# Both filter products in one operation, and twenty weight tiles beside the first batch's length-47 steps

## The chip, the cores and the metric

The kernel runs on one core of a Trainium2 chip. A core has five engines with instruction streams of their own: TensorE (PE, with its weight loads listed as PEld), VectorE (DVE), ScalarE (ACT), GpSimd (POOL) and SyncE (SP). They work on tiles in SBUF, a memory of 128 partitions; TensorE writes its results to banks of a second memory, PSUM. Transfers between these and the main memory (DMA) are issued from the queues of SP, ACT and POOL. The metric is the device time of one execution in microseconds (us); the time of before is the median of six runs.

## The reference

Two blocks follow each other on x of shape (8, 3008, 256), all in float32 except the four mixer weights, which arrive as float64.

```python
X = np.fft.rfft(x, axis=1)                      # 1505 frequencies along the sequence
Y = X * (filt_r + 1j * filt_i)[None]            # a complex filter for each frequency and channel
x = np.fft.irfft(Y, n=3008, axis=1).astype(np.float32)
xt = x.transpose(0, 2, 1)
h = np.maximum(xt @ w_tok1, 0.0) @ w_tok2       # token mixing: 3008 -> 256 -> 3008
u = x + h.transpose(0, 2, 1)
h2 = np.maximum(u @ w_ch1, 0.0) @ w_ch2         # channel mixing: 256 -> 1536 -> 256
out = (u + h2).astype(np.float32)
```

## The kernel before

**The transform.** The length 3008 is split as 64 x 47. A forward transform of a batch has twelve units of the length-64 part (`a_unit`, a matrix product with a table `wa`) and then 32 steps of the length-47 part, one for each k2. In a step `b_unit(k)` multiplies by the step's table and leaves 128 rows of frequencies in PSUM: real parts in rows 0 to 63, imaginary parts in rows 64 to 127. Then DVE applies the filter, and `bi_unit(k)` applies the inverse table of length 47 and sends the result through ACT (the copy t at L520) to the scratch tensor `g_tmp` in main memory. The inverse of the length-64 part is folded into the mixer: `w_tok1` is multiplied by that inverse when it is loaded (`w1`), and the second token product adds it by way of `wai`.

**The filter products.** A complex product needs re*fr, im*fr, -im*fi and re*fi. The tile `filt` holds filt_r in part 0 (rows 0 to 63, doubled into rows 64 to 127) and filt_i in part 1. In the first batch DVE makes p1 = ps * fr over 128 rows (L502), and p2 with the halves swapped: p2[re] = -ps[im] * fi (L503) and p2[im] = ps[re] * fi (L504). `bi_unit` then multiplies both p1 and p2 by the same inverse table and lets PSUM add them. In the later groups, of two batches each, DVE adds p1 and p2 itself.

**The order.** The order of all work is written out by hand. The first batch is transformed alone (`dft(GROUPS[0])`), before there is anything to mix; the other seven go in groups beside the mixer of the batches before. The first batch's `a_unit`s take the first 20 us, then come transposes on DVE, then the 32 steps. ACT doubles the filter of the next pair of steps at every odd step (`filt_double`, L226), ahead of the copy t of that step. The filter of a pair (c) is six transfers, on POOL's queue except for c = 1 and 2, which go through SP's.

**The weights.** 40 tiles of float64 weights are turned to float32: 12 of w_tok1 (tiles 0 to 11, 512 columns), 16 of w_tok2 (tiles 12 to 27, 377 columns), 12 of the channel weights. Each tile is a generator with stages: start the load; an ACT operation (L246); four DVE operations (L248, L249, L251, L253), which split a number into a top and a rest; and then the sum of the two. For w_tok1 and the first `BY_PE` tiles of w_tok2 PE forms the sum, as two products with the table `wai_t` or the identity (L285, L286), and ACT copies it out (L288); for the others DVE adds (L274). `convert()` ends the oldest tile, gives the next one its ACT operation and starts loads up to six tiles ahead (`fill`). A buffer of a load comes free when the DVE operations of its old tile are done.

Before the change `convert()` is called 12 times beside the 32 steps and 16 times after them. Between these, after the sixth w_tok2 tile, come the token sums of batch 0 (`token_sums`, 96 instructions, L566), which need all of w1 and all of the batch read back from `g_tmp` (`t4_load`, L560). After the last w_tok2 tile the mixer begins: `token_relu` (L572), `u_part` (L583, L588), `v_steps` (L601), then the loop `mix`.

Of the kernel before, what the change touches and what calls it, by code (L numbers as in the profile page):

```python
# [10 lines left out]
FP32 = mybir.dt.float32  # L11
I64 = mybir.dt.int64
U32 = mybir.dt.uint32
AF = mybir.ActivationFunctionType
# [29 lines left out]
MT = 6  # L44
NG = 8
PARTS = (0, 64, 112)
BY_PE = 6
EARLY = 12
GROUPS = ((0,), (1, 2), (3, 4), (5, 6), (7,))

# [74 lines left out]
def kernel(  # L125
# [64 lines left out]
    wai_t = glob.tile([P, P], FP32, name="wai_t")  # L190
    ident = h1p.tile([P, P], FP32, tag="h1", name="ident")

    filts = [glob.tile([P, 2, KC, D], FP32, name="filt%d" % i) for i in range(FB)]
    w1 = glob.tile([P, A, DT], FP32, name="w1")

# [12 lines left out]
    def filt_load(c, first):  # L208
        t, k0 = filts[c % FB], c * KC


        q = nc.gpsimd if first and c not in (1, 2) else nc.sync
        for src, i, p0 in ((filt_r, 0, 0), (filt_i, 1, HALF)) + (() if first else ((filt_r, 0, HALF),)):
            q.dma_start(t[p0:p0 + A, i], raw(src, k0, [[64 * D, A], [D, KC], [1, D]]))
            lo = p0 + 32
            if k0 == 0:
                q.dma_start(t[lo:lo + A, i, 0, :], raw(src, 32, [[64 * D, A], [1, D]]))
            k = max(k0, 1)

            for j0, n in ((0, 16), (16, A - 1 - 16)):  # L220
                q.dma_start(t[lo + j0:lo + j0 + n, i, k - k0:KC, :],
                            raw(src, 64 * (j0 + 1) - k, [[64 * D, n], [-D, k0 + KC - k], [1, D]]))

    def filt_double(c):
        t = filts[c % FB]
        nc.scalar.copy(out=t[HALF:P, 0], in_=t[0:HALF, 0])  # L226

# [8 lines left out]
    def halves(st, n, pair):  # L238

        words = [st.bitcast(t).rearrange("p (n w) -> p n w", w=2)[:, 0:n] for t in (U32, FP32)]  # L240
        lo, hi, hi_f = words[0][:, :, 0], words[0][:, :, 1], words[1][:, :, 1]
        top, rest = (v[:, 0:n] for v in pair)
        top_i, rest_i = top.bitcast(U32), rest.bitcast(U32)


        nc.scalar.activation(out=top, in_=hi_f, func=AF.Copy, scale=2.0 ** -112)  # L246
        yield
        nc.vector.tensor_scalar(out=top_i, in0=top_i, scalar1=3, scalar2=None, op0=ALU.logical_shift_left)  # L248
        nc.vector.scalar_tensor_tensor(out=top_i, in0=hi, scalar=0x80000000, in1=top_i,  # L249
                                       op0=ALU.bitwise_and, op1=ALU.bitwise_or)  # L250
        nc.vector.tensor_scalar(out=rest_i, in0=top_i, scalar1=0xFF800000, scalar2=None, op0=ALU.bitwise_and)  # L251

        nc.vector.scalar_tensor_tensor(out=rest, in0=lo, scalar=2.0 ** -52, in1=rest, op0=ALU.mult, op1=ALU.mult)  # L253
        yield top, rest
# [9 lines left out]
    def rounded(st, n, parts, late):  # L264
        if late:

            pair = (p1p.tile([P, 512], FP32, tag="p1", name="top"), p2p.tile([P, 512], FP32, tag="p2", name="rest"))
        else:
            pair = spare_pair()
        h = halves(st, n, pair)  # L270
        yield next(h)
        top, rest = next(h)
        for src, dst in parts:
            nc.vector.tensor_tensor(out=dst, in0=src(top), in1=src(rest), op=ALU.add)  # L274
# [17 lines left out]
    def w1_load(i):  # L292
        st = stage(512)
        rows = moe_w_tok1.rearrange("(n2 n1) t -> n2 n1 t", n1=N1)
        q = nc.sync if i < EARLY else nc.gpsimd
        last = 2 * i + 2 == A
        if last:
            nc.gpsimd.memset(st.bitcast(U32)[HALF:P, 512:1024], 0)
        for h in range(2):
            n = 1 if last and h else 2  # L300
            lo = h * A + 2 * i
            q.dma_start(st[h * HALF:(h + 1) * HALF, 0:n * DT].rearrange("p (a t) -> p a t", t=DT),
                        rows[:, lo:lo + n, :])
        yield

        h = halves(st, 512, spare_pair())
        yield next(h)
        on_chip(wai_t, *next(h), 512, [(lambda v: v, w1[:, 2 * i:2 * i + 2, :].rearrange("p a t -> p (a t)"))])

    def w2_load(i):  # L310

        t, g = divmod(i, N2 // NG)
        n = NG * N1

        more = g + 1 < N2 // NG
        st = stage(512)
        nc.gpsimd.dma_start(st[:, 0:n + more], moe_w_tok2[ts(t, P), ds(g * n, n + more)])
        yield
        dst = w2[:, t].rearrange("p (a h n2) -> p h n2 a", h=2, n2=HALF)[:, :, ds(g * NG, NG), :]

        def some(h, nh, w):
            return (lambda v: bass.AP(tensor=v.tensor, offset=v.offset + h * A, ap=[v.ap[0], [A, nh], [N1, NG], [1, w]]),
                    dst[:, h:h + nh, :, 0:w])

        parts = [some(0, 2, A)] if more else [some(0, 1, A), some(1, 1, A - 1)]
        if i < BY_PE:
            h = halves(st, n + more, spare_pair())
            yield next(h)
            on_chip(ident, *next(h), n + more, parts)
        else:  # L330
            yield from rounded(st, n + more, parts, False)
# [23 lines left out]
    def wc2_load(i):  # L355
# [5 lines left out]
        def tile_of(dh):  # L361
# [9 lines left out]

    tiles = ([w1_load(i) for i in range(A // 2)] + [w2_load(i) for i in range(TC * N2 // NG)]
             + [wc1_load(c * (DC // 512), False) for c in range(DH)] + [f(i) for f, i in LAST])
    begin, copy, end = iter(tiles), iter(tiles), iter(tiles)

    def advance(it):
        s = next(it, None)
# [6 lines left out]

    def convert():

        ended[0] += 1
        while behind and behind[0][0] < ended[0] - 2:
            behind.pop(0)[1]()
        advance(end)  # L390
        advance(copy)
        fill(6)
# [46 lines left out]
    def dft(bs):  # L439
# [44 lines left out]
        def b_unit(k):  # L484
            tag = ("b", "pg")[k % 2] if first else free_bank()
            if not first:
                held.append(tag)
            ps = bank(tag).rearrange("p (b d) -> p b d", b=2)[:, 0:nb, :]
            t2 = turned[:, k, :].unsqueeze(1) if first else t2s[k // KC][:, k % KC]
            nc.tensor.matmul(ps, wbs[k // WC][0:P if first else KR, k % WC, 0:P], t2, start=True, stop=True)  # L490
            re, im = slice(0, HALF), slice(HALF, P)
            t = filts[k // KC % FB]
            fr = t[:, 0, k % KC, :].unsqueeze(1).to_broadcast([P, nb, D])
            fi = t[im, 1, k % KC, :].unsqueeze(1).to_broadcast([HALF, nb, D])
            p1 = p1p.tile([P, 2 if first else nb, D], FP32, tag="p1", name="p1")
            if first:
                p1, p2 = p1[:, 0:1], p1[:, 1:2]
                prods[k] = (p1, p2)
            else:
                p2 = p2p.tile([P, nb, D], FP32, tag="p2", name="p2")  # L500
                prods[k] = (p1,)
            nc.vector.tensor_tensor(out=p1, in0=ps, in1=fr, op=ALU.mult)  # L502
            nc.vector.scalar_tensor_tensor(out=p2[re], in0=ps[im], scalar=-1.0, in1=fi, op0=ALU.mult, op1=ALU.mult)  # L503
            nc.vector.tensor_tensor(out=p2[im], in0=ps[re], in1=fi, op=ALU.mult)  # L504
            if not first:
                nc.vector.tensor_tensor(out=p1, in0=p1, in1=p2, op=ALU.add)

        def bi_unit(k):

# [1 line left out]
            ps = bank("acc" if first else held.pop(0)).rearrange("p (b d) -> p b d", b=2)[:, 0:nb, :]  # L511
            parts = prods.pop(k)
            for i, p in enumerate(parts):
                nc.tensor.matmul(ps[0:KR], wbs[k // WC][:, k % WC, P:], p, start=(i == 0), stop=(i == len(parts) - 1))  # L514
            c, r = divmod(k, KC)
            if r == 0:
                where, tag = (p2p, "p2") if first and c % 3 == 2 else (t3p, "t3")
# [14 lines left out]
        yield  # L532
        if first:
            filt_double(0)
        for k in range(K2 + 1):
            if k < K2:
                b_unit(k)
# [8 lines left out]
                        table_load(k // KC + 4)  # L546
                if first and k % KC == KC - 1 and k + 1 < K2:
                    filt_double(k // KC + 1)
            if k >= 1:
                bi_unit(k - 1)  # L550
            yield
# [241 lines left out]
    with tc.manual_schedule():  # L793
        nc.sync.dma_start(wa0, wa0_d)
        nc.vector.memset(turned[:, A:K2, :], 0.0)
        for t in filts:
            nc.vector.memset(t, 0.0)
        rounds = 0
        second = dft(GROUPS[1])
        for i, _ in enumerate(dft(GROUPS[0])):  # L800
            if i == 0:
# [8 lines left out]
                    for t, src in ((wa, wa_d), (wai, wai_d), (ident, ident_d)):  # L810
                        nc.scalar.dma_start(t, src)
            elif k >= 0:
                if (k + 1) * (A // 2) // K2 > k * (A // 2) // K2:
                    convert()
                    rounds += 1

                if 19 <= k < 25:
                    t4_load(0, k - 19, 0, PARTS[1])
                elif k == 25:
                    next(second)  # L820
                elif k in (30, 31):
                    for c in range(3):
                        t4_load(0, 3 * (k - 30) + c, PARTS[1], PARTS[2])
# [3 lines left out]
        both = wcp.tile([P, 2, JP, 7, P], FP32, tag="wc", name="wc")  # L827

        chan.extend((both[:, 0], both[:, 1]))
        for i in range(rounds, A // 2 + TC * N2 // NG):  # L830
            convert()
            if i - rounds < XB:
                next(second)
            if i == A // 2 + BY_PE - 1:
                sum_up()
                acc = token_sums(0)
        h1s[0] = token_relu(acc)
        for dh in range(DH):
            convert()
# [59 lines left out]
```

## Time and profile before

| | |
|---|---|
| median of 6 runs | 2577.82 us (2576.47 to 2579.71) |
| profiled execution | 2579.51 us, its span 2577.7 us |
| busy over the span | PE 97%, DVE 70%, ACT 27%, POOL 20% |
| mean granted TensorE clock | 0.994 |
| first length-47 step to the last one's copy | 30.5 to 108.4 us |
| token sums of batch 0 | 122.6 to 143.5 us |
| first sums of the mixer (v, L601) | 155.0 us |

The profile is one execution on the chip. Engine rows with 40 digits give the busy share of 40 equal slices in tenths; a table by stages gives each engine's busy time and instruction count in a window, the granted clock, the mean busy share of 16 DMA engines and GB/s. A row of a group names a line, an engine, an operation, output and input with their shapes and a count; behind it stand busy us, mean ns of one, and the engine's idle time before these instructions with what ended it. A row of the timeline gives start, length, engine, line and instruction, and in brackets the idle time before it. Waits are listed as the waiting engine and line, what it waited for, us in all, times, and the longest.

### The profile page before, as it was taken

How to read it: one execution, taken by the hardware profiler on the slowest of the kernel's cores; microseconds unless marked ns; L12 is line 12 of the kernel's file. 1: busy time of each engine (PE TensorE's matmuls, PEld its weight loads, DVE VectorE, ACT ScalarE, POOL GpSimd, SP SyncE). 2: the span in 40 equal slices, each digit the busy share in tenths (PEclk: the TensorE clock that was granted, in tenths of full speed). 3: DMA queues.
4: the chain of work that ended last, by engine and by line, in shares of the span. 5: the costliest groups of instructions: out<-in, count | busy, mean ns of one | idle time of the engine just before them, and what ended most of it. 6: DMA issues, size and time to landing. Idle time of an engine off the chain costs nothing.

```text
span 2577.7 us, 31460 instructions
## 1 busy us (share of the span) xinstructions
PE 2502.7 (97%) x10952; PEld 1999.6 (78%) x10952; DVE 1815.4 (70%) x3458; ACT 691.9 (27%) x1347; POOL 527.5 (20%) x968
## 2 busy tenths in 40 slices
PE   6979999999999999999999999999999999999998
PEld 3557666888778777887888777788888888888887
DVE  7897888466585887745665888746678576647676
ACT  3533222122222222222221222213222122212222
POOL 4563111111211121112121111211211121211212
PEclk8999999999999999999999999999999999999999
DMA  9964333212322232203232233212222121100000
GB/s 212 231 205 146 96 104 96 86 58 92 99 85 63 81 92 62 80 25 92 88 93 73 79 85 86 82 28 65 85 82 77 51 62 53 25 9 8 17 12 21
DMA packets 153775, 205.21 MB, mean 80 GB/s; under 512 B 34128, under 2 KB 105074, under 8 KB 153616
## 3 DMA queue, kind: packets, MB, share of 16 engines
q1 hardware_dynamic: 82752, 114.46, 15.8%
q0 software_dynamic: 30912, 41.12, 6.7%
q10 hardware_dynamic: 39952, 47.61, 5.8%
q8 instruction: 87, 1.43, 0.2%
q14 instruction: 72, 0.59, 0.1%
HBM read 131.23 MB, written 71.83 MB: 79 GB/s over the span
## 4 chain that ended last, share of the span: by engine, by line
PE 79%; DVE 13%; DMA 3%; issue 2%; ACT 1%; POOL 1%; SPq 0%; ACTq 0%; DVEq 0%; POOLq 0%
PE ps_po L657 27%; PE ps_pg L623 16%; PE ps_pg L639 12%; PE ps_acc L583 4%; PE ps_acc L566 3%; PE ps_b L583 3%; PE ps_b L566 2%; DVE t L601 2%; DVE hh L601 2%; PE ps_acc L588 2%; PE ps_acc L514 2%; PE ps_b L430 2%; PE ps_b L490 2%; DVE u L601 1%; PE ps_acc L490 1%
## 5 line engine op out<-in xcount | busy, mean ns | idle before, releaser
L601 DVE TENSOR_TENSOR hh<-ps_pg,s 128x512 f32<-128x512 f32 (+3 forms) x864 | 482.0, 585 | 613.1 <-ACT s L626 612.5
L702 POOL DMA_DIRECT2D out_dram<-r x757 | 409.8, 550 | 1950.8 <-ACT hh L644 925.9
L644 ACT ACTIVATE hh<-hh 128x512 f32<-128x512 f32 (+1 forms) x576 | 347.9, 621 | 1113.9 <-DVE hh L601 1113.9
L657 PE MATMUL ps_po<-t,wc 128*128 128x256 f32 (+1 forms) x2304 | 537.0, 376 | 5.7 <-DVE t L601 4.7
L657 PEld LDWEIGHTS ps_po<-t,wc 128*128 128x128 f32 x2304 | 435.2, 190 | 132.2 <-issue 52.1
L657 PE MATMUL ps_po<-hh,wc 128*128 128x256 f32 (+1 forms) x1728 | 413.2, 375 | 2.9 <-POOL wc L340 1.5
L623 PE MATMUL ps_pg<-v,wc 128*128 128x256 f32 (+1 forms) x1728 | 413.4, 375 | 0.2
L657 PEld LDWEIGHTS ps_po<-hh,wc 128*128 128x128 f32 x1728 | 327.4, 190 | 42.1 <-POOL wc L340 1.9
L623 PEld LDWEIGHTS ps_pg<-v,wc 128*128 128x128 f32 x1728 | 326.9, 190 | 40.8 <-DVE v L601 3.2
L639 PE MATMUL ps_pg<-u,wc 128*128 128x256 f32 (+1 forms) x1152 | 293.3, 377 | 5.1 <-DVE hh L601 4.7
L601 DVE TENSOR_TENSOR t<-t,hh 128x256 f32<-128x256 f32 (+1 forms) x576 | 242.0, 420 | 19.8
L639 PEld LDWEIGHTS ps_pg<-u,wc 128*128 128x128 f32 x1152 | 215.8, 190 | 41.7 <-DVE hh L601 14.9
L601 DVE TENSOR_TENSOR s<-ps_pg,hh 128x512 f32<-128x512 f32 (+1 forms) x288 | 196.1, 681 | 30.3 <-DVE hh L601 0.5
L601 DVE TENSOR_TENSOR t<-hh 128x512 f32<-128x512 f32 (+1 forms) x288 | 192.4, 668 | 0.6 <-ACT hh L644 0.6
L623 PE MATMUL ps_pg<-u,wc 128*128 128x256 f32 (+1 forms) x576 | 169.8, 376 | 0.0
L639 PE MATMUL ps_pg<-v,wc 128*128 128x256 f32 (+1 forms) x576 | 169.1, 375 | 0.0
L626 ACT COPY s<-ps_pg 128x256 f32<-128x256 f32 (+1 forms) x288 | 106.0, 368 | 156.1 <-PE ps_pg L623 152.9
L639 PEld LDWEIGHTS ps_pg<-v,wc 128*128 128x128 f32 x576 | 108.5, 190 | 13.5 <-DVE s L601 0.4
L623 PEld LDWEIGHTS ps_pg<-u,wc 128*128 128x128 f32 x576 | 102.8, 191 | 19.4 <-issue 11.0
L583 PE MATMUL ps_acc<-w,h 128*128 128x512 f32 (+1 forms) x228 | 106.3, 588 | 3.5 <-DVE w L274 2.8
L514 PE MATMUL ps_acc<-p,wb 128*96 128x256 f32 (+1 forms) x256 | 96.6, 478 | 13.2 <-ACT t L520 7.3
L566 PE MATMUL ps_b<-t,w 128*128 128x256 f32 x384 | 83.8, 380 | 1.3 <-ACT t L520 1.3
(104 smaller groups left out, 2267.6 us busy)
## 6 DMA issues: line engine op xcount, KB each, us to landing
g_tmp<-t ACTq DMA_DIRECT2D x128, 192.0 KB
out_dram<-r POOLq DMA_DIRECT2D x698, 32.0 KB, 1.8
x<-in_x_dram SPq DMA_DIRECT2D x173, 128.0 KB
z_tmp<-t ACTq DMA_DIRECT2D x84, 256.0 KB
t<-z_tmp SPq DMA_DIRECT2D x112, 192.0 KB
t<-g_tmp SPq DMA_DIRECT2D x42, 512.0 KB
wb<-wbi_t SPq DMA_DIRECT2D x80, 224.0 KB
filt<-in_filt_r_dram SPq DMA_DIRECT2D x130, 48.0 KB
```

The lines of the kernel that those rows point to most:

```text
L430: nc.tensor.matmul(ps, wa0 if b == 0 else wa, xs.pop((b, c)).rearrange("p a d -> p (a d)"), start=True, stop=True)
L490: nc.tensor.matmul(ps, wbs[k // WC][0:P if first else KR, k % WC, 0:P], t2, start=True, stop=True)
L514: nc.tensor.matmul(ps[0:KR], wbs[k // WC][:, k % WC, P:], p, start=(i == 0), stop=(i == len(parts) - 1))
L566: nc.tensor.matmul(acc[:, t, :], w1[:, a, ts(t, P)], t4[b, a // TC4][:, a % TC4, :], start=(a == 0 and t == 0), stop=(a == A - 1 and t == ...
L583: nc.tensor.matmul(ps[:, 0:w], h1[:, t, ts(dh, P)], w2[:, t, ds(m * 512, w)], start=(t == 0), stop=False)
L601: nc.vector.tensor_tensor(out=out, in0=in0, in1=in1, op=op)
L623: nc.tensor.matmul(ps[:, 0:hw], chan[0][:, jp, n, :], mov, start=True, stop=True)
L626: nc.scalar.copy(out=s[:, 0], in_=g[0][:, 0, 0:hw])
L639: nc.tensor.matmul(ps[:, 0:hw], chan[0][:, jp, n, :], mov, start=True, stop=True)
L644: nc.scalar.activation(out=hs, in_=hs, func=AF.Relu)
L657: nc.tensor.matmul(po[i][:, j, 0:hw], chan[1][:, jp, n, :], mov, start=(jp == 0 and first == 1), stop=(jp == JP - 1 and last == 1))
L702: q.dma_start(rows[g, e, :, ds(h * A + 4 * m, n)], blocks[ts(g, CW), h, e, 0:n])
```

## The change

1. In the first batch one DVE operation makes both filter products: ps, read twice by a broadcast, times both parts of the filter tile, over 128 rows and 2 x 256 columns. For that filt_i is loaded into rows 0 to 63 like filt_r, and `filt_double` copies both parts (64x1024 instead of 64x512).
2. The swap and the sign that p2 had are put into a second inverse table, `turn_i`, that ACT makes from the first with two operations for each pair of steps (`table_turn`), ahead of the copy t of every odd step. `bi_unit` multiplies the second part by it. `turn_i` shares its buffer with the tile `s` of the mixer.
3. The four DVE operations of a tile are split into two stages of two operations. Beside the 32 steps 20 tiles (`IN_B`) are converted, in half stages, instead of 12; eight are left for after the loop.
4. PE forms the sum for 4 tiles of w_tok2 instead of 6. The token sums are issued before the conversions that follow the loop, not after the sixth of them, and the two `a_unit`s of the second group before the token sums.
5. The filter of c = 2 is loaded through POOL's queue instead of SP's.

```diff
-BY_PE = 6
+BY_PE = 4
+IN_B = 20
...
-        q = nc.gpsimd if first and c not in (1, 2) else nc.sync
-        for src, i, p0 in ((filt_r, 0, 0), (filt_i, 1, HALF)) + (() if first else ((filt_r, 0, HALF),)):
+        q = nc.gpsimd if first and c != 1 else nc.sync
+        for src, i, p0 in ((filt_r, 0, 0), (filt_i, 1, 0 if first else HALF)) + (() if first else ((filt_r, 0, HALF),)):
...
     def filt_double(c):
         t = filts[c % FB]
-        nc.scalar.copy(out=t[HALF:P, 0], in_=t[0:HALF, 0])
+        nc.scalar.copy(out=t[HALF:P], in_=t[0:HALF])
+
+    turn_i = sp.tile([P, 4, WC, KR], FP32, tag="s", name="turn_i")
+
+    def table_turn(g, wb):
+        wi, to = wb[:, :, P:], turn_i[:, g % 4]
+        nc.scalar.copy(out=to[0:HALF], in_=wi[HALF:P])
+        nc.scalar.activation(out=to[HALF:P], in_=wi[0:HALF], func=AF.Copy, scale=-1.0)
...
         nc.vector.scalar_tensor_tensor(out=top_i, in0=hi, scalar=0x80000000, in1=top_i,
                                        op0=ALU.bitwise_and, op1=ALU.bitwise_or)
+        yield
         nc.vector.tensor_scalar(out=rest_i, in0=top_i, scalar1=0xFF800000, scalar2=None, op0=ALU.bitwise_and)
...
-    begin, copy, end = iter(tiles), iter(tiles), iter(tiles)
+    begin, copy, middle, end = (iter(tiles) for _ in range(4))
...
     def convert():
+        advance(middle)
+        convert_end()
+
+    def convert_end():
         ended[0] += 1
...
             if first:
-                p1, p2 = p1[:, 0:1], p1[:, 1:2]
-                prods[k] = (p1, p2)
-            else:
-                p2 = p2p.tile([P, nb, D], FP32, tag="p2", name="p2")
-                prods[k] = (p1,)
+                nc.vector.tensor_tensor(out=p1, in0=ps.to_broadcast([P, 2, D]), in1=t[:, :, k % KC, :], op=ALU.mult)
+                prods[k] = (p1[:, 0:1], p1[:, 1:2])
+                return
+            p2 = p2p.tile([P, nb, D], FP32, tag="p2", name="p2")
+            prods[k] = (p1,)
...
-                nc.tensor.matmul(ps[0:KR], wbs[k // WC][:, k % WC, P:], p, start=(i == 0), stop=(i == len(parts) - 1))
+                wi = turn_i[:, k // WC % 4, k % WC] if i else wbs[k // WC][:, k % WC, P:]
+                nc.tensor.matmul(ps[0:KR], wi, p, start=(i == 0), stop=(i == len(parts) - 1))
...
         if first:
             filt_double(0)
+            table_turn(0, wbs[0])
...
                 if first and k % KC == KC - 1 and k + 1 < K2:
                     filt_double(k // KC + 1)
+                    table_turn(k // KC + 1, wbs[k // KC + 1])
...
             elif k >= 0:
-                if (k + 1) * (A // 2) // K2 > k * (A // 2) // K2:
-                    convert()
-                    rounds += 1
+                while half < 2 * IN_B * (k + 1) // K2:
+                    if half % 2:
+                        convert_end()
+                    else:
+                        advance(middle)
+                    half += 1
...
-        for i in range(rounds, A // 2 + TC * N2 // NG):
+        for _ in range(XB):
+            next(second)
+        acc = token_sums(0)
+        for _ in range(A // 2 + TC * N2 // NG - IN_B):
             convert()
-            if i - rounds < XB:
-                next(second)
-            if i == A // 2 + BY_PE - 1:
-                sum_up()
-                acc = token_sums(0)
         h1s[0] = token_relu(acc)
```

More of the change, by code (lines that the diff above doesn't have):

```diff
@@ L270, in rounded @@
         h = halves(st, n, pair)
+        yield next(h)
         yield next(h)
@@ L307, in w1_load @@
         yield next(h)
+        yield next(h)
         on_chip(wai_t, *next(h), 512, [(lambda v: v, w1[:, 2 * i:2 * i + 2, :].rearrange("p a t -> p (a t)"))])
@@ L327, in w2_load @@
             h = halves(st, n + more, spare_pair())
+            yield next(h)
             yield next(h)
@@ L504, in b_unit @@
             nc.vector.tensor_tensor(out=p2[im], in0=ps[re], in1=fi, op=ALU.mult)
-            if not first:
-                nc.vector.tensor_tensor(out=p1, in0=p1, in1=p2, op=ALU.add)
+            nc.vector.tensor_tensor(out=p1, in0=p1, in1=p2, op=ALU.add)
         def bi_unit(k):
@@ L797 @@
             nc.vector.memset(t, 0.0)
-        rounds = 0
+        half = 0
         second = dft(GROUPS[1])
```

## The prediction

> **What bounds the kernel now.** I read the page first, then the first 260 us by stage, then the waits, the chain of waits and each engine's timeline there. The page says where a change to the first batch can pay:
>
> ```profile
> span 2577.7 us, 31460 instructions
> ...
> PE   6979999999999999999999999999999999999998
> ...
> DVE  7897888466585887745665888746678576647676
> ...
> DMA  9964333212322232203232233212222121100000
> ```
>
> From about 200 us on TensorE (PE) is full; this work the change does not touch, so it can only start earlier or later. The profiled execution took 2579.51 us, 1.8 more than its span, and lies 1.7 above the median of 2577.82; I work in differences and subtract them from the median. The stages of interest are the loop of 32 length-47 steps (30.5 to 108.4) and the stretch from it to the mixer's first sums (155.0). The columns are length, then busy time of PE, PEld, DVE, ACT and POOL, granted clock, DMA share, GB/s:
>
> ```profile
> 30.50:108.40 77.90, 69.08 (x234) 40.94 (x235) 66.55 (x145) 32.78 (x68) 46.62 (x85) 0.94 0.89 226
> 108.40:155.00 46.60, 42.94 (x158) 28.55 (x156) 40.94 (x87) 17.96 (x32) 15.32 (x29) 0.96 0.78 202
> ```
>
> In the loop PE, DVE and the DMA engines are all above 85%; ACT and POOL are not. What ends the second stretch is in PE's timeline:
>
> ```profile
> 122.60 20.88 PE L566 MATMUL ps_b<-t,w 128*128 128x256 f32 x96
> 144.17 1.12 PE L583 MATMUL ps_acc<-w,h 128*128 128x512 f32 x2 [0.69 <-ACT h L572]
> 148.07 1.58 PE L583 MATMUL ps_acc<-w,h 128*128 128x512 f32 x2 [2.78 <-DVE w L274]
> ```
>
> The token sums (L566) are done at 143.5, but the next product waits until 148.07 for DVE, which converts w2 tiles without a gap from 112.55 to 148.0. So after the loop it is DVE's sixteen w2 tiles that set the time, 39.7 us (108.4 to 148.07).
>
> **The products.** Busy time and mean ns of one, from the groups of lines; the last row is the second group's product, of the new product's size, also PSUM times SBUF with a broadcast operand:
>
> ```profile
> L502 DVE TENSOR_TENSOR p<-ps_b,filt 128x256 f32<-128x256 f32 x16 | 6.7, 421 | 3.9 <-ACT filt L226 1.5 <-issue 1.4 <-ACT t L520 0.8
> L503 DVE SCALAR_TENSOR_TENSOR p<-ps_b,filt 64x256 f32<-64x256 f32 x16 | 6.8, 426 | 3.2 <-DMA filt<-in_filt_i_dram 2.8
> L504 DVE TENSOR_TENSOR p<-ps_b,filt 64x256 f32<-64x256 f32 x16 | 6.7, 418 | 0.2
> L502 DVE TENSOR_TENSOR p<-ps_acc,filt 128x512 f32<-128x512 f32 x2 | 1.4, 692 | 3.7 <-PE ps_acc L490 3.7
> ```
>
> Start to start the three take 1.33 us; one at 0.692 and a gap of 0.03 takes 0.72. Over 32 steps 42.6 becomes 23.0: 19.6 us of DVE saved. If the broadcast of the PSUM operand ran no faster than the three did, nothing would be saved; I take 0.72, the row of equal size.
>
> **The tiles beside the steps.** A w1 tile costs DVE 2.27 (49.93 to 52.19), a w2 tile finished by PE 1.84 (112.55 to 114.39), one finished by DVE's addition 2.62 (137.43 to 140.05). Before, the loop's DVE holds 42.6 + 12 x 2.27 = 69.8; after, 23.0 + 27.2 + 4 x 1.84 + 4 x 2.62 = 68.1. So eight tiles come in for the products' saving and DVE's loop time stays the same. Halving a tile puts at most about 1.2 us of it in a row between two products; it costs no instruction, and I count nothing. PE gets 4 x 1.27 = 5.1 us more in the loop (a 377-column pair takes 0.635, 113.00 to 113.64). Dense, its loop is 32 x 1.30 + 12 x 1.72 + 5.1 = 67.3, below DVE's.
>
> **After the loop.** DVE keeps eight w2 tiles, 8 x 2.62 = 21.0. PE needs the g_tmp round trip, then 20.9 of token sums and 0.7 for the relu. The round trip: a g_tmp store landed in 2.15 (36.93 to 39.10) and six SP issues at 0.45 take 2.7, so with a load's landing 6 at least; at most the 14.2 that lay between 108.4 and 122.60, when six of the ten w2 loads that were left (377 KB each) were issued beside it. After the change two are left, so I take 7.8, near the low end. The stretch to the first w2 product becomes 7.8 + 20.9 + 0.7 = 29.4 (27.6 to 35.8) in place of 39.7: 10.3 saved (3.9 to 12.1). What is late next is the token sums; DVE ends 8 us ahead of them. The mixer's start (155 to 215, PE 49 of 60 us busy) is a chain of DVE, POOL and x loads that the change only shifts.
>
> **What the loop pays.** The waits inside it, in us, times and longest (the last is SP's queue):
>
> ```profile
> PEld ps_acc L514 <- ACT t L520: 17.3, 23, 3.6
> ...
> ACT filt L226 <- DMA filt<-in_filt_r_dram: 10.2, 5, 3.3
> PE ps_acc L514 <- ACT t L520: 7.3, 6, 3.2
> ...
> SPq L221 <- DMA g_tmp<-t: 6.6, 1, 6.6
> ```
>
> *ACT.* The filter copy grows from 64x512 (0.616) to 64x1024. ACT's rows 96x256 at 0.368 and 128x512 at 0.586 give 0.85 ns per element, so about 1.05: 16 x 0.43 = 6.9. The table turn adds two operations of 64x192 at about 0.33: 10.6. Together 17.5 us. Eight more tile starts and six more on-chip copies make ACT 59 us of 78 instead of 33. ACT is in order: the filter copy and turn stand ahead of the copy t L520, for which PE's only "acc" bank waits, and the filter copy now also waits for filt_i, which is issued about 1.7 us behind filt_r. Five waits by 1.7 are 8.5, of which DVE's L503 already paid 2.8. Exposed: between 0 (ACT has 45 us to spare) and 17.5; I take 3.5, since filters mostly come in time in the second half.
>
> *DMA.* Eight loads of 377 KB, 3.09 MB, move into the loop. At its 226 GB/s that is 13.7 us. A share of 0.89 leaves some 2.2 MB free (226/0.89 x 0.11 x 77.9), so 0.9 MB, 3.5 us, is what I take, between 0 (only tiles 18 and 19 are wanted that were not already issued in the loop) and 13.7.
>
> The Trainium skill (DMA: Bandwidth & Descriptors, Specifications) puts the HBM limit of one core near 358 GB/s. By it the eight loads would be an estimated 8.6 us, all of it inside the spare rate, and the DMA term zero. The trace speaks against that: the engines were at a share of 1.05 with 233 GB/s between 108.4 and 122.6.
>
> *Queues.* The eight loads go on POOL's queue between the filter loads, 0.57 each, 4.6 us; POOL is busy 46.6 of 77.9, but each also waits for the DVE half that frees its buffer, and the next filter load is queued behind it. If all eight hold a filter load up by 0.57 and a half of 1.2, and each delay reaches PE, that is 14 us; if POOL's 31 idle us take them, 0. I take 0, the end nearer to a queue 60% busy, and leave the other to the range. The third filter pair (c = 2) goes from SP to POOL: six issues of 0.53 while POOL idles from 19 to 34. On SP they waited 6.6 us and PE then stood 3.25 us (to 41.73) for ACT's copy behind that filter. I count 3.0 saved (0 to 3.25).
>
> The Trainium skill (DMA: Bandwidth & Descriptors, Issuing engines are not separate DMA queues) says that starting transfers from another engine saves only sequencer time. By it this move gives PE nothing and the sum would be 3 us less; the wait of 6.6 us is a queue's, not an engine's, which is why I do not follow it here.
>
> The new shared buffer "s" is first wanted by L626 after 155 us, long after the last use of the turned table: no cost. The two w2 tiles taken from PE after the loop are in the sums above.
>
> **Sum.** Loop +3.5 (ACT) + 3.5 (DMA) - 3.0 (c = 2) = +4.0; stretch after it -10.3; total -6.3: 2577.8 - 6.3 = 2571.5 us.
>
> **Rivals.** *Bytes:* the loop grows by the full 13.7, less the 3 from c = 2, and the gain after it is given back: 2577.8 + 10.7 - 10.3 = 2578.2, no change. For it speaks the share near 1 from 50 to 70 us; against it the 0.86 from 78 us on, where most of the w2 loads would go. *ACT becomes the bound (slower):* each odd step is longer by all of its filter copy and turn. Loop +17.5 + 3.5 - 3.0 = 18.0, less 10.3: 2585.5. It decides from an exposure of 59% of ACT's added work (10.3 of 17.5) when the other two terms cancel. For it: 24.6 us of PE waits for L520 exist already; against it: much of that is the pipe of one bank, and ACT idles over half the loop. *The broadcast product doesn't save:* at 1.33 a step DVE's loop is 87.7, +18 on 69.8, and the time about 2585, as in the last case; little speaks for it. *All hidden (better):* loop -3, stretch -12.1: 2562.7.
>
> **How the numbers follow.** About 0.2% (5.2 us) is what a measurement can tell from no change. Forecast with the better case 0.56 (below 2572.6); bytes, or half-exposed ACT, 0.26 (2572.6 to 2583.0); ACT bound 0.14 and dear product 0.04, slower, 0.18. The forecast's own range is 2564 to 2575; the whole reaches from the better case, 2562, to most of the slower one, 2584.
>
> **What would show it.** Right: L502's product near 0.69 us and no L503 or L504 in the loop; the last of its products 0 to 8 us later than before; token sums begun within 10 us of that; L583 waiting for h L572 and not for w L274; v L601 some 6 us before 155.0. Wrong: a loop that ends after 119, with ACT above 85% or long waits of L226, or POOL's filter loads waiting behind w2 loads; or t from g_tmp landing as late after the loop as before.

## The result, and the profile after

The changed kernel took 2583.88 us (median of 17 runs, 2580.73 to 2585.89) against 2577.3 for the kernel before beside it: a ratio of 1.0023 with a 95% interval of 1.0016 to 1.0029. Where 6.3 us less was forecast, it is 6 us slower, and the interval excludes no change. The profiled execution took 2584.97 us, its span 2582.9, 5.2 more than before's.

The stages first, in the same columns as before (length, busy time of PE, PEld, DVE, ACT and POOL, granted clock, DMA share, GB/s): the loop, then the stretch to the mixer's first sums.

```profile
30.50:122.50 92.00, 76.76 (x257) 46.03 (x258) 62.45 (x115) 55.72 (x109) 50.87 (x92) 0.95 0.87 226
122.50:164.30 41.80, 32.70 (x129) 24.92 (x128) 28.80 (x58) 9.24 (x17) 13.32 (x25) 0.88 0.62 149
```

DVE's work in the loop fell from 66.55 to 62.45 us, by more than worked out (69.8 to 68.1, with gaps). But the loop is 14.6 us longer: its last copy t ends at 123.05, half a us behind this window, where before it ended at 108.48. DVE is now busy for only 68% of it. ACT went from 32.78 to 55.72. The DMA engines move the same 226 GB/s, so the loop carries 20.8 MB where it carried 17.6. After it PE is idle for 9 of 42 us, at a granted clock of 0.88.

The product itself is what it was taken for, in the groups of lines (busy us and mean ns of one):

```profile
L516 DVE TENSOR_TENSOR p<-ps_b,filt 128x512 f32<-128x512 f32 x16 | 11.0, 689 | 5.1 <-PE ps_b L508 2.4 <-issue 1.4 <-DMA filt<-in_filt_r_dram 1.0
```

Next the waits between 30 and 122 us (total, times, longest). PE waits 15.0 us for the copy t, now L539, in place of 7.3, and its weight loads 23.6 in place of 17.3. The two overlap in time, so their sums, 38.6 and the prediction's 24.6, are not time that was lost. ACT's filter copy waits for filt_i:

```profile
PEld ps_acc L533 <- ACT t L539: 23.6, 21, 4.6
PE ps_acc L533 <- ACT t L539: 15.0, 10, 4.2
DVE both L258 <- ACT both L256: 14.0, 9, 5.3
...
ACT filt L228 <- DMA filt<-in_filt_i_dram: 7.6, 2, 4.9
```

The chain of waits shows what one of these is made of (start, length, what):

```profile
98.00 0.55 POOL st L330
98.54 0.66 POOL filt L216
...
101.33 7.20 DMA filt<-in_filt_i_dram
...
108.71 1.04 ACT filt L228
109.77 0.35 ACT turn_i L235
110.12 0.36 ACT turn_i L236
...
110.51 0.38 ACT t L539
```

A w2 load (L330) goes out on POOL's queue ahead of the filter of c = 14; the last piece of that filter is under way for 7.20 us; then come copy and turn, and only then the copy t of the step before, which needs neither. PE stood 4.22 us for it, to 110.93.

After the loop, rows of the timeline (in brackets the idle time before a row):

```profile
123.08 0.31 ACTq L544 DMA_DIRECT2D g_tmp<-t  x1
...
123.34 1.02 PE L448 MATMUL ps_acc<-x,wa 128*128 128x512 f32 x2
...
127.78 2.67 SPq L581 DMA_DIRECT2D t<-g_tmp  x6
...
132.78 23.93 PE L587 MATMUL ps_b<-t,w 128*128 128x256 f32 x96 [8.41 <-ACT both L256]
...
157.40 1.98 PE L604 MATMUL ps_acc<-w,h 128*128 128x512 f32 x4 [0.69 <-ACT h L593]
```

The profile puts the 8.41 us down to an ACT operation whose output the sums don't use. What they do need comes through `g_tmp`: the last store goes out at 123.08, SP issues the six loads that read it back from 127.78 to 130.45, and the sums begin 2.3 us later.

The first product with w2 waits for h, not for DVE, as forecast; but it comes 34.4 us after the loop's last copy where 29.4 was forecast, and at 157.40 where before had 148.07.

### The profile page after: what moved, and what is told of

Its sections match the earlier page's. It is cut to its first block, busy times and chain, and to the rows that moved or that the text cites. A ratio compares the mean times of both kernels' runs of the same rounds, so it can differ in the third digit from the quotient of the medians.

```text
span 2582.9 us, 31406 instructions
## 1 busy us (share of the span) xinstructions
PE 2499.1 (97%) x10944; PEld 2001.0 (77%) x10944; DVE 1795.5 (70%) x3396; ACT 708.0 (27%) x1377; POOL 529.7 (21%) x974
## 4 chain that ended last, share of the span: by engine, by line
PE 81%; DVE 11%; DMA 3%; ACT 2%; issue 2%; POOL 0%; ACTq 0%; SPq 0%; DVEq 0%; POOLq 0%
PE ps_po L678 28%; PE ps_pg L644 16%; PE ps_pg L660 12%; PE ps_acc L604 4%; PE ps_b L587 3%; PE ps_acc L587 3%; PE ps_b L604 2%; DVE t L622 2%; DVE hh L622 2%; PE ps_acc L609 2%; PE ps_acc L533 2%; PE ps_b L448 2%; PE ps_b L508 1%; PE ps_acc L508 1%; PE ps_b L533 1%
## 5 line engine op out<-in xcount | busy, mean ns | idle before, releaser
L678 PEld LDWEIGHTS ps_po<-hh,wc 128*128 128x128 f32 x1728 | 327.6, 190 | 38.6 <-ACT s L647 0.8
L533 PE MATMUL ps_acc<-p,wb 128*96 128x256 f32 (+1 forms) x192 | 80.6, 501 | 19.6 <-ACT t L539 15.0
```

The costliest lines, as they stand in the source:

```text
L533: nc.tensor.matmul(ps[0:KR], wi, p, start=(i == 0), stop=(i == len(parts) - 1))
L678: nc.tensor.matmul(po[i][:, j, 0:hw], chan[1][:, jp, n, :], mov, start=(jp == 0 and first == 1), stop=(jp == JP - 1 and last == 1))
```

## The experiments

In each table, "loop" is the start of the last product with the inverse table in the profiled execution (before 107.42, changed kernel 122.05; 106.99 and 121.6, in two expectations, are the starts of that step's first product), "sums" the start of the token sums (122.60, 132.78), "mixer" the first product with channel weights (155.99, 164.52). The ratio is to the kernel before, which ran beside each on the same chip, with its interval; the chips differ between rows, so ratios are compared and not medians. Single profiles differ: all_oldprod and fin_old are one kernel and gave 109.8 and 110.7 for the loop; inb16_acc2_sp_warm and fin_one are another and gave 110.6 and 109.3, and 154.1 and 151.2 for the mixer.

**Terms taken back one at a time**, each from the changed kernel.

*w2_sp*, the w2 loads of tiles 12 to 25 on SP's queue in place of POOL's:

```diff
-        nc.gpsimd.dma_start(st[:, 0:n + more], moe_w_tok2...
+        (nc.sync if i < 14 else nc.gpsimd).dma_start(st[:, 0:n + more], moe_w_tok2...
```

> The changed kernel with one thing altered: the w2 loads that start beside the steps (tiles 12 to 25) are issued from SP's queue, so that no filter load stands behind one on POOL's. After the change the loop's last product began at 121.6 us and its step at 106.11 waited 4.2 us for a filter pair that was issued behind two w2 loads. Queue theory: the filter loads come in time, that wait goes, the loop ends 6 to 10 us sooner (112 to 116) and the time is 4 to 8 us below the changed kernel's 2583.9. ACT theory (the filter copy and the table turn stand ahead of the copy t): less than 2 us change, PE still waits for t about 1.7 us at every second odd step. Bytes theory (the DMA engines are full): no change, the same bytes in another queue.

*turn4*, table turns for the first 4 of 16 pairs only:

```diff
     def table_turn(g, wb):
+        if g >= 4:
+            return
```

> The changed kernel with the table turn made only for the first 4 of 16 pairs of steps; the later pairs use the old contents, so 24 ACT operations of 0.35 us (8.5 us) are left out. ACT theory: the copy t comes 0.71 us sooner in each of 12 odd steps, the loop ends 5 to 9 us sooner and the time falls by about as much. Queue theory: PE waits shift from ACT's own work to ACT's wait for filters; at most 3 us.

*oldprod*, the 20 tiles and the new order, but the three old product operations, one filter half copied and no turned table:

```diff
-                nc.vector.tensor_tensor(out=p1, in0=ps.to_broadcast([P, 2, D]), in1=t[:, :, k % KC, :], op=ALU.mult)
+                p1, p2 = p1[:, 0:1], p1[:, 1:2]
...
+            nc.vector.tensor_tensor(out=p1, in0=ps, in1=fr, op=ALU.mult)
```

> The changed kernel with the three old products and the filter copy of before, without the turned table; the 20 tiles in halves, the order after the loop and c = 2 on POOL stay. DVE's loop is 42.6 + 45.1 = 88 us, so it should end no sooner than 119. ACT theory: ACT is free again, so DVE alone sets it, 119 to 122. Queue theory: the delays of filters come on top of it or are hidden beneath DVE: 121 to 128. If it ends near 122 like the changed kernel, the fused product gave nothing in this loop.

*nobytes*, the loads of tiles 18 to 25 left out; these tiles are made from the data of tiles 12 and 13:

```diff
+        if 6 <= i < 14:
+            st = kept[i % 2]
```

> The changed kernel without eight of its w2 loads: tiles 18 to 25 are made from the staged data of tiles 12 and 13, so 3.09 MB and eight issues on POOL's queue are left out of the loop, while all arithmetic stays. Bytes theory: at 226 GB/s the loop ends 8 to 14 us sooner than the changed kernel's last product at 122, so 108 to 114. Queue theory: as with the loads on SP's queue (116.3), 114 to 117. ACT theory: ACT's chain of filter copy, turn and copy t remains, no less than 116.

*actfree*, turn4 and the copy of the real half alone; *floor*, actfree and nobytes together:

```diff
-        nc.scalar.copy(out=t[HALF:P], in_=t[0:HALF])
+        nc.scalar.copy(out=t[HALF:P, 0], in_=t[0:HALF, 0])
```

> The changed kernel with the turned table made for 4 of 16 pairs only and the filter copy of part 0 alone (64x512, filt_i's second copy left out): ACT's added 17.5 us fall to 2.8 and the copy waits for filt_r alone. ACT theory: the loop ends 10 us or more sooner than 122, near 110 to 112. Bytes or queue theory: the waits pass from ACT's copies to the filters' arrival and the loop ends at 115 to 119, as it did with the turn alone left out (118.1).

> Both of the last two at once: eight w2 loads, 12 of 16 table turns and the second filter copy left out. If bytes and ACT together make up the 14 us by which the loop grew, it ends at 100 to 108 (PE's dense work is 67 us, DVE's 68, from 30.5). If it ends above 111, something else holds the loop.

*upper*, filt_i loaded to rows 64 to 127 as before, two copies of 64x512:

```diff
+        nc.scalar.copy(out=t[HALF:P, 0], in_=t[0:HALF, 0])
+        nc.scalar.copy(out=t[0:HALF, 1], in_=t[HALF:P, 1])
```

> The changed kernel with the imaginary filter loaded to partitions 64 to 127, as before the change; ScalarE then copies the real half up and the imaginary half down, two operations of 64x512 (about 2 x 0.62 us) in place of one of 64x1024 (1.04). Theory A (both filter halves landing on the same 64 partitions slows the filters' arrival): the loop's last product moves from 122 us to 116 or earlier and the span falls by 4 or more. Theory B (the loop is late because the filter loads stand behind w2 loads on POOL's queue, and ScalarE's chain stands behind the filters): the loop ends within 3 us of 122, no change beyond 2 us.

*acc2*, two banks for the steps' sums:

```diff
-            ps = bank("acc" if first else held.pop(0))
+            ps = bank(("acc", "po3")[k % 2] if first else held.pop(0))
```

> The changed kernel with the products of odd and even steps summed in two PSUM banks instead of the one bank acc (the on-chip tiles use three banks in place of four). Theory A (ScalarE's copy t out of the one bank is what PE waits for, 33 us in all, because the copy stands behind filter copies and turns): the waits of PE for ACT t fall to under 10 us and the loop's last product comes at 112 us or earlier, the time about 2575. Theory B (the copies only pass on that filters and table turns come late, which the next product waits for anyway): the waits move to DVE's and ACT's waits for the filter, the loop ends after 117 us, the time within 2 us of 2583.

| kernel | loop | sums | mixer | median us | ratio |
|---|---|---|---|---|---|
| w2_sp | 116.3 | 128.9 | 160.6 | 2582.71 | 1.0019 [1.0009, 1.0028] |
| turn4 | 118.1 | 131.8 | 163.3 | 2584.11 | 1.0022 [1.0013, 1.0032] |
| oldprod | 118.2 | 127.2 | 158.3 | 2583.07 | 1.0015 [1.0006, 1.0025] |
| nobytes | 114.4 | 128.7 | 159.1 | 2581.27 | 1.0014 [1.0004, 1.0025] |
| actfree | 114.9 | 129.4 | 159.7 | 2581.23 | 1.0013 [1.0004, 1.0023] |
| floor | 115.3 | 132.6 | 164.1 | 2581.48 | 1.0009 [0.9999, 1.0019] |
| upper | 119.6 | 130.5 | 161.7 | 2583.14 | 1.0018 [1.0009, 1.0028] |
| acc2 | 119.6 | 133.2 | 164.6 | 2583.59 | 1.0015 [1.0006, 1.0025] |

Each shortens the loop by 2 to 8 us, none brings it near 107, and they do not add: floor, which is actfree and nobytes at once, has neither's loop bettered. Nobytes is a weaker test than it was meant to be: freed buffers let later loads move up, and its loop still carried 19.9 MB (84.4 us at 236 GB/s). By the ratios the times move by 3.6 us at most, and the intervals of these runs overlap, so the table orders the loops and not the times. Part of what a loop gains is lost again behind it: SP begins to read `g_tmp` back 4.7 us after the last store in the changed kernel, 10.6 in nobytes and 13.9 in floor. In acc2 the waits of PE and its loads for the copy t sum to 12.0 us instead of 38.6, and the loop ended only 2.4 us sooner. Its largest wait in the loop was

```profile
ACT filt L228 <- DMA filt<-in_filt_i_dram: 16.4, 8, 6.4
```

so that the waits for ACT seem to have been largely waits for filters, passed on.

Two of these runs tell what the one operation saves where ACT has about the same work (columns as above; oldprod, then actfree):

```profile
30.50:118.60 88.10, 78.46 (x256) 44.77 (x257) 80.14 (x177) 40.37 (x81) 51.17 (x92) 0.95 0.93 237
30.50:115.30 84.80, 74.56 (x256) 45.44 (x257) 61.37 (x115) 41.52 (x85) 51.13 (x92) 0.96 0.92 239
```

With 18.8 us less on DVE the loop's last product comes 3.3 us sooner. That is in single profiles, and actfree leaves out most of the ACT work that the one operation needs.

**Fewer tiles beside the loop**: `IN_B = 12` and `IN_B = 16`.

> The changed kernel with 12 tiles beside the steps (in halves) in place of 20, so 16 w2 tiles follow the loop, as before the change; fused product, turned table, filter copy and c = 2 on POOL stay. If the fused product is a gain by itself, DVE's loop is 23 + 27 = 50 us and the loop ends well before 108: queue and bytes theories say 98 to 104, since w2 loads then hardly mix with the filters. ACT theory says 106 or later, because all of ACT's added work (17.5 us) is still there. After the loop DVE needs 16 tiles, 4 x 1.84 + 12 x 2.62 = 39 us, so with a loop end of 102 the first w2 product comes near 142 and the time is about 2571; with 108, about 2577.

> The changed kernel with 16 tiles beside the steps in place of 20: 1.55 MB fewer and four tiles less of DVE and ACT in the loop, twelve w2 tiles on DVE after it, 12 x 2.62 = 31.4 us. PE's on-chip tiles are all done in the loop, so none stands behind the token sums, as it did with 12. Bytes theory: the loop ends 6 to 7 us sooner, near 115; the stretch after it is 34 to 36 us as in the changed kernel (34.9), set by the round trip and the token sums. Time 3 to 7 us below the changed kernel's, 2577 to 2581. ACT theory: the loop ends at 119 or later, and the time stays above 2581.

With 16 tiles the loop ended at 114.1, the mixer began at 156.5 and the time was 2579.74, ratio 1.0007 [0.9998, 1.0017]. With 12, the number of before, the loop ended at 112.6, still 5.2 after before's, though its DVE was busy for only 47.5 of 82.5 us: DVE was not what held it. So of the 14.6 us by which the last product moved, 5.2 come with the product change and the move of c = 2, without one more tile, and 9.4 with the eight tiles (1.5 with the first four, 7.9 with the others; single profiles). The time, 2614.75 (1.0137 [1.0122, 1.0153]), is another matter. The token sums now stand ahead of tiles whose sums PE must form. ACT waited 27.0 us to copy these out, in order ahead of its relu h and of the operations that start DVE's last tiles (DVE waited 24.9 for ACT):

```profile
123.40 22.86 PE L587 MATMUL ps_b<-t,w 128*128 128x256 f32 x96 [5.04 <-DMA t<-g_tmp]
...
177.99 2.07 PE L604 MATMUL ps_acc<-w,h 128*128 128x512 f32 x2 [26.36 <-ACT h L593]
```

So the new order needs all of PE's tiles inside the loop: the parts of the change hang together.

**The slow token sums.** *warm* is the changed kernel with eight products that nobody reads, just before the sums:

```diff
+        warm = bank("po0")
+        for _ in range(8):
+            nc.tensor.matmul(warm, ident, w1[:, 0:2, :]..., start=True, stop=True)
         acc = token_sums(0)
```

> The changed kernel with eight idle products (128x512, into a bank that nobody reads) on PE just ahead of the token sums, so that PE isn't idle while the stored sums come back. Theory A (the token sums took 23.93 us in place of 20.88 because PE had stood 8.4 us and its granted clock fell): the token sums take about 21 us, the first product after them comes 3 us earlier for the same landing of t4, the time 2 to 3 us lower. Theory B (the clock falls for another reason, or the products hold PE up): the token sums stay at 23 us or start later, the time stays at 2583 or rises.

Measured: 2580.47 us, 3.4 below the changed kernel (2.8 by the ratios, 1.0012 [1.0003, 1.0022] against 1.0023): the sign stays, about half of the loss is gone. PE's timeline:

```profile
123.76 7.03 PE L858 MATMUL ps_po<-w,ident 128*128 128x512 f32 x16
132.52 20.96 PE L587 MATMUL ps_b<-t,w 128*128 128x256 f32 x96 [1.73 <-ACT both L256]
```

The sums start at the same moment and take 20.96 in place of 23.93. The term is shown in the trace; by the times alone it is not, since the intervals overlap.

**The remedies together, and the products apart.** *inb16_acc2_sp_warm* is 16 tiles with acc2, w2_sp and warm; *acc2_sp_warm* the same with 20; *all_oldprod* has 16 tiles, all remedies and the old products of oldprod. *fin_one* and *fin_old* are the first and the last of these again, side by side. (The text on fin_old names tiles 12 and 13 for the loads on SP's queue; they are those of tiles 12 to 25, as in the others.)

> All remedies together: 16 tiles beside the loop in place of 20, two banks for the steps' sums, the w2 loads of tiles 12 to 25 on SP's queue, eight idle products ahead of the token sums. If the three causes add up (queue, one bank, cold clock) the loop ends near 108 us, the first product after the token sums comes near 142 us and the time is about 2572, 5 below before. If they are one cause seen three times, it gives what 16 tiles alone gave, 2579 to 2580. Not below that if SP's queue delays the t4 loads by as much as it frees the filters.

> The changed kernel with its 20 tiles, and the three remedies: two banks for the steps' sums, w2 loads of tiles 12 to 25 on SP's queue, eight idle products ahead of the token sums. Theory A (the remedies carry the gain, whatever the number of tiles): loop's last product at 113 or earlier, time about 2577. Theory B (twenty tiles are too many for a loop whose ScalarE and filter queue are shared with them): loop's last product at 116 to 119, time 2579 to 2581, that is w2_sp less the 3 us of the warm clock.

> The kernel with 16 tiles and all remedies (inb16_acc2_sp_warm), but with the three old product operations, the filter copied by half and no turned table. Theory A (the one-operation product gains once ScalarE's chain and the queue are out of the way): DVE is busy above 95% of the loop, which ends 4 us or more after 110.6, and the time is 3 or more above 2577.2. Theory B (what the product saves on DVE, ScalarE's copies and turns take back whatever else is done): the loop ends within 2 us of 110.6 or earlier, and the time is within 2 us of 2577.2.

> all_oldprod again, in five rounds (three old product operations, 16 tiles in halves beside the loop, two banks, w2 loads of tiles 12 and 13 on SP's queue, eight idle products ahead of the token sums). Theory A (this is really faster than before): ratio about 0.999 with an interval below 1. Theory B (chance): 1.000.

> inb16_acc2_sp_warm again, in five rounds: the same but for the one-operation product, the turned table and the wider filter copy. Theory A (ScalarE pays back at least what VectorE saves): 1 to 2 us above fin_old. Theory B (the product is worth something): below fin_old.

| kernel | tiles, products | loop | mixer | median us | ratio |
|---|---|---|---|---|---|
| inb16_acc2_sp_warm | 16, one operation | 110.6 | 154.1 | 2577.21 | 0.9994 [0.9984, 1.0003] |
| fin_one | the same | 109.3 | 151.2 | 2577.25 | 0.9996 [0.9987, 1.0005] |
| all_oldprod | 16, three operations | 109.8 | 152.2 | 2575.30 | 0.9988 [0.9978, 0.9997] |
| fin_old | the same | 110.7 | 153.0 | 2576.08 | 0.9992 [0.9983, 1.0000] |
| acc2_sp_warm | 20, one operation | 115.3 | 157.9 | 2584.02 | 1.0018 [1.0009, 1.0028] |

The remedies work with 16 tiles and not with 20 (acc2_sp_warm's profile is of its fastest run, 2578.56; the ten go up to 2589.82, and why they spread so isn't known). Against before, all_oldprod's interval lies below 1 and that of the same kernel as fin_old reaches 1.0000: a gain of some 2 us is likely, not shown. The loops of fin_old, fin_one and acc2_sp_warm:

```profile
30.50:110.70 80.20, 72.67 (x247) 41.83 (x246) 71.14 (x159) 35.62 (x74) 43.89 (x79) 0.97 0.95 237
30.50:109.80 79.30, 71.14 (x249) 44.18 (x250) 53.34 (x98) 50.20 (x103) 43.98 (x79) 0.95 0.95 246
30.50:115.70 85.20, 74.42 (x257) 46.18 (x258) 61.23 (x114) 54.09 (x109) 43.61 (x79) 0.95 0.95 241
```

With one operation DVE has 17.8 us less to do and ACT 14.6 more, and the last product comes 1.4 us sooner; in the other pair it comes 0.7 later. So as a whole the product change gains next to nothing in the loop; this pair doesn't tell whether DVE's time was off the path or ACT's added work took it back. By the ratios the three operations are even the faster ones, by 1.5 and 1.0 us; the intervals overlap, so no gain is seen and a small one isn't excluded. What the three loops share is a DMA share of 0.95. With 20 tiles the loop carries 20.5 MB, with 16 and the same product 19.5: 1 MB more is 4 us at 241 GB/s, of the 6.0 by which it ends later. That fits a loop held by its transfers and is no test of it.

**The third filter pair.** *before_c2* is the kernel before with `c != 1` for `c not in (1, 2)`; *c2_acc2* adds two banks to that.

> The kernel before with one edit: the third filter pair (c = 2) issued by POOL in place of SP. My sum gave it -3.0 (0 to -3.25). Theory A: the loop's last product comes about 3 us before 106.99 and the time falls by 1 to 3 us. Theory B (the loop is bound by DVE and the steady arrival of filters and w1 tiles, so that a stall at 41 us is made up by 107): the third step pair comes earlier, the end of the loop does not, no change of the time within 1 us.

> The kernel before with two edits: the third filter pair on POOL's queue and two banks for the steps' sums; 12 tiles, old products, old order after the loop. If the gain of fin_old comes from these two alone: about 0.999. If before's loop is bound by VectorE (66.6 of 77.9 us busy, 42.6 of it products), the two banks add nothing to the third pair's move: 0.9994, as before_c2.

The ninth step came at 48.9 and 48.7 in place of 50.83, the seventeenth at 66.6 and 69.8 in place of 70.98. So both are 2 us ahead at first, but only before_c2 keeps a lead, 4.3 us halfway and 2.8 at the end: the loop's last product came at 104.6 in the one and 108.0 in the other (before 107.4). The ratios are 0.9994 [0.9984, 1.0005] and 0.9993 [0.9984, 1.0002]. A gain of 1 to 2 us fits both and isn't separated from none.

## Why the prediction was wrong

**Right.** The product at 0.69 (0.692 forecast), the copy of 64x1024 at 1.044 (1.05), the turns at 0.35 and 0.36 (0.33). DVE's loop work fell; the first w2 product waits for h and no longer for DVE.

**The step that failed first: the loop.** I forecast +4.0, it was +14.6. As the third filter pair, taken as -3.0, gave 2.8 at the loop's end in before_c2 and nothing in c2_acc2, the other terms, +7.0, were some 15 to 17. By inb12 the loop is 5.2 us longer without one more tile, where ACT's term and the filter pair made +0.5; the eight tiles add 9.4, where I had 3.5. I had shown that DVE's work stayed the same, and from three engines above 85% took it that the loop would too. The chain of waits of the kernel before over the same 78 us, which I did not read there, names other work:

```profile
by line: DMA filt<-in_filt_r_dram 22.2%; PE ps_acc L514 16.7%; DMA filt<-in_filt_i_dram 14.8%; POOL filt L221 8.9%; issue 7.7%; POOL filt L214 5.3%; PE ps_b L490 4.3%; PE ps_pg L490 3.8%; DMA g_tmp<-t 2.8%; PE ps_po L285 2.8%; ACT filt L226
```

The same row of the changed kernel, over its 92 us:

```profile
by line: DMA filt<-in_filt_i_dram 14.2%; PE ps_acc L533 12.2%; DMA filt<-in_filt_r_dram 12.1%; DMA st<-in_moe_w_tok_dram 11.2%; ACT filt L228 5.8%; issue 5.7%; PE ps_po L298 4.7%; PE ps_po L297 4.7%; POOL filt L223 3.6%; ACT both L256 3.4%;
```

In the kernel before, the filters' transfers and their issue on POOL are 51% of the chain; no line of DVE stands in what the row shows, down to 2.8%. In the changed kernel the weight loads are 11.2% of it (10.3 us) and the wider filter copy 5.8% (5.3 us). So the time that the product saved was worth little there (3.3 us of 18.8, actfree against oldprod), and what the change added went onto the path. By terms:

- *Bytes*, taken as +3.5 because a share of 0.89 left 2.2 MB. The loop carried 3.2 MB more, about the eight loads' 3.09, and the rate did not rise at all: the growth is that of the upper bound, 13.7. With the other obstacles gone the rate came to 246 GB/s at a share of 0.95, so some room was there, but not beside these queues and waits. That bytes alone are the cause isn't shown: inb12's loop is 5.2 us longer with only 0.5 MB more than before's, nobytes gave back 7.6, and a loop that is long for another reason also lets more loads in.
- *POOL's queue*, taken as 0 of 14: w2_sp gave back 5.8 us of the loop, in one profile.
- *ACT*, taken as +3.5 of 17.5: actfree gave back 7.1. As the terms do not add, their shares stay open; the loop has several waits of one size, and whichever is taken away the next is close behind.

The Trainium skill (DMA: Bandwidth & Descriptors, Issuing engines are not separate DMA queues) would make w2_sp's edit worth only sequencer time. The runs don't speak against it: POOL's busy time in the loop fell by 7.5 us (50.87 to 43.42), more than the 5.8 that the loop gained, and the time (1.0 us by the ratios, intervals overlapping) decides nothing.

**The second: the stretch after the loop**, forecast at 29.4 and measured at 34.4 from the last copy's end (the text on inb16 has 34.9, from 122.5). The round trip was 9.7 where I took 7.8 of 6 to 14.2; in the runs with the new order it took 7.6 (oldprod) to 16.3 us (floor). The other 3.0 is a term I did not have: with the tiles gone from between loop and sums, PE idles 8.4 us. In the changed kernel's stages from 124.4 on, the granted clock (first of the last three columns) follows:

```profile
124.40:132.80 8.40, 0.02 (x1) 0.05 (x1) 7.91 (x17) 3.10 (x6) 2.54 (x5) 0.75 1.02 298
132.80:136.20 3.40, 3.40 (x8) 2.77 (x9) 3.19 (x8) 0.55 (x1) 1.70 (x4) 0.50 1.04 186
136.20:140.00 3.80, 3.80 (x13) 3.08 (x13) 3.63 (x8) 0.55 (x1) 2.23 (x5) 0.66 1.06 244
140.00:144.00 4.00, 4.00 (x20) 3.54 (x19) 3.76 (x9) 0.69 (x1) 2.97 (x6) 1.00 1.04 254
```

The first sums run at half clock, 8 products in 3.4 us, where warm's first 3.5 us hold 16. The Trainium skill (TensorE: Matmul & The Clock Gate, What's actually happening) says that an idle window of some 3.4 us halves the clock, and that about as long a busy one restores it. The trace agrees on the fall. The return came some 6 us after the sums began: half clock for 3.4 us, and a mean of 0.66 over the next 3.8, which is an estimated 2.6 us more at half clock. Warm shows the price: 3 us. In the kernel before, the work of six w2 tiles stood in this place (PE busy for 14.0 of the 14.2 us from 108.4 to 122.6, at a clock of 1.00) and hid both the round trip and the clock; moving it into the loop removed the cover.

**The third: a lead is not kept.** I passed what is saved before the mixer on to the end in full. At the first product with channel weights before_c2, fin_old and fin_one are 2.8, 3.0 and 4.8 us ahead of before; at the next products with w2, at 199.26 in before, they are 0.5 behind, level, and 1.6 ahead. Each has lost about 3 us. Between these points PE waits in fin_one mostly for channel weights and DVE's hh (3.3 and 3.2 us in all), in before mostly for x (6.2). The changed kernel's delay is kept: 8.5 at the same first product, 8.2 at the second point, 9.6 at 447.54. (2.9 of that goes by 518.10, because the profiled execution of before paused for 2.87 us at 472.81, which the profiles of fin_old, fin_one and the changed kernel don't do.) So, as an estimate from these three profiles, the forecast's -6.3 would have come out nearer to -3 even if the terms had been right.

**Rivals.** The result, 2583.88, lies near the slower rival's 2585.5, in part by luck: its loop, +18.0, was 3.4 us too long and the stretch after it 5.1 too short, and ACT's work was exposed, but not alone. The bytes rival's loop, +10.7, was 3.9 too short, and it too took the whole gain of 10.3 after it, where 5.2 was left.

## What to carry to other kernels

Before work is moved into a stage, read the chain of waits of that stage alone: freeing an engine that isn't on it buys little, whatever its busy share. A DMA share below 1 need not be room for more transfers (here 0.89, and the rate stayed at 226 GB/s); price added bytes at the rate that the stage has now, as the dear end. And ask what the moved work was hiding where it stood: here a round trip through main memory, and a clock that falls when PE idles.

## What the runs showed of the hardware that was not expected

The clock's price on a dependent stretch: 8.4 us without PE work cost 3 us in the next 24 (23.93 against warm's 20.96). In every profile with 3 us or more of idling right before the sums they took 22.5 to 24.0 us, in every one without it 20.9 to 21.0; eight useless products took the 3 us back.

A DMA share near 1 stands for no fixed rate: in the four stages above it is 1.02 to 1.06, and the rate 298, 186, 244 and 254 GB/s. My division of 226 GB/s by 0.89 to find the spare rate had no ground.
